# Gated mix of dilated attention and a gated MLP: another order of the first loads, ones for the early matmuls, and another split of the last tile

## The chip, the cores and the metric

The kernel runs on one core of one Trainium2 chip. The metric is the time of one execution on the device in microseconds (us). The time before is the median of three executions. Times inside an execution come from one profiled execution and are counted from the start of its span, that is from its first instruction.

## The reference

Everything is in bfloat16, for 2048 rows of 1024 columns (x). Two branches are computed from x and mixed by a gate.

```python
x = A_x
g = _sigmoid((x * gate_w).sum(-1, keepdims=True))
a = _A_ref(x, A_wqkv, A_wo)                  # 32 heads, 8 keys at a distance of 2, softmax, then wo
b = _B_ref(x, B_w_in, B_w_sp, B_b_sp, B_w_out)
return g * a + (1 - g) * b
...
z = _gelu(jnp.einsum('bsd,df->bsf', x, w_in))       # w_in: 1024 x 3584
z1 = z[..., :Fh].copy()
z2 = _layernorm(z[..., Fh:], axis=-1)
g = jnp.einsum('ts,bsf->btf', w_sp, z2) + b_sp[None, :, None]
return jnp.einsum('bsf,fd->bsd', z1 * g, w_out)
```

## The kernel before

The rows are 16 tiles of 128, the 1024 columns of x are 8 k tiles of 128. TensorE goes through these stages, one after the other: the second half of z (z2) for the first column blocks, q, k and v (L447), the rest of z2 (L232), the first half of z (L483), the spatial product g (L497) in four chunks, and after the chunks the two output products, attention (L510) and MLP (L520). The attention itself is done by VectorE beside the matmuls. PSUM has eight banks, taken in turn; ScalarE and VectorE copy results out of them.

The order of instructions on every engine is that of the program text: the scheduler is switched to manual, and each engine's queue executes in order. A small class, Beat, counts the columns that TensorE has multiplied and places VectorE's attention steps and some DMAs by that count. All DMAs before the change are issued from SP's queue; each issue takes the queue some tenths of a microsecond, and each DMA uses one of eight semaphores in turn, so that it also waits for the DMA that had the semaphore before.

The steps that the change touches are the first and the last.

At the start, matmuls on x need x transposed (columns on the partitions). For row tiles 2 to 15 the DMA transposes (L412). For row tiles 0 and 1 the plain tiles are loaded (L405, one DMA of 128 x 1024 each) and TensorE transposes them (L247): for each row tile two banks of four 128x128 transposes, each bank copied to xT in two parts, one by VectorE (L251) and one by ScalarE (L253). Behind the x tiles SP issues the eight k tiles of w_in for the first 1024 columns of z2 (L407, 256 KB each), then the transposing loads. At the very start VectorE clears a tile named warm (L87), and TensorE does six 128x512 matmuls on it whose result nobody reads (L92). Then comes the quad (z2_quad): both row tiles by both 512-column blocks in four PSUM banks, with the k tile as the outer loop, so that the work on a k tile starts when this tile has landed. ScalarE applies GELU to the four banks after the last k tile (L237). The row tiles 2 to 15 follow with the first column block, then v's weights are reordered (L218, L219), and the qkv stage starts with four weight blocks that SP loads at L205.

At the end, final_chunk(3) computes row tiles 12 to 15. For each column part of a row tile, attn_mm does 8 matmuls, mixer_mm 14, and combine does one operation on ScalarE (L527, attention times the gate, into one of two buffers asb) and one on VectorE (L528). The row tiles up to 14 have two parts of 512 columns and one store (L550); row tile 15 has parts of 512, 256 and 256 columns and a store after each (L548).

The constant that the change uses is one of four that the framework sets up in every program, with a one-column memset on GpSimd before the barrier at the start of the kernel (line L585 of the profile).

Of the kernel before, what the change touches and what calls it, by code (L numbers as in the profile page):

```python
# [11 lines left out]
BF = mybir.dt.bfloat16  # L12

P = 128
# [11 lines left out]
FH = 1792  # L26
NF = FH // P
ZC = 512
# [23 lines left out]
def kernel(  # L52
# [13 lines left out]
    nc = tc.nc  # L66
# [4 lines left out]
    sm = ctx.enter_context(tc.tile_pool(name="small", bufs=1))  # L71
    psum = ctx.enter_context(tc.tile_pool(name="psum", bufs=8, space=bass.MemoryType.PSUM))
# [4 lines left out]
    def reg(off, n):  # L77
        return arena[:, off:off + n]
# [4 lines left out]
    z1_d = dpool.tile([4, P, NF * 512], BF, name="z1_d")  # L83
    o_d = dpool.tile([S, D], BF, name="o_d")

    warm = sm.tile([P, 512], BF, name="warm")
    nc.vector.memset(warm[:], 0.0)  # L87

    def warm_up(n):
        pw = psum.tile([P, 512], F32, name="pw", tag="ps")  # L90
        for _ in range(n):
            nc.tensor.matmul(pw[:], warm[:, 0:P], warm[:], start=True, stop=True)  # L92

    ident = sm.tile([P, P], BF, name="ident")
    make_identity(nc, ident[:])
# [3 lines left out]
    for jh in range(2):  # L99
        for w in range(W):  # L100
            n = min(8, max(0, 14 - 2 * w - 8 * jh))
# [5 lines left out]
    gl_s = sm.tile([P, 16], F32, name="gl_s")  # L107
# [14 lines left out]
    xn = reg(A_OFF, 2 * D).rearrange("p (i d) -> p i d", i=2)  # L122
    z2 = reg(Z_OFF, 16 * FH).rearrange("p (i f) -> p i f", i=16)
    xT = reg(X_OFF, KT * S).rearrange("p (k s) -> p k s", k=KT)
# [10 lines left out]
    asb_slots = [reg(A_OFF + 14336 + r * 1024, 1024).bitcast(F32) for r in range(2)]  # L135
    w2 = reg(CD_OFF, KT * W2P).rearrange("p (k c) -> p k c", k=KT)
# [14 lines left out]
    x_v = x2.rearrange("(i q) d -> q i d", q=P)  # L151
# [3 lines left out]
    win_v = B_w_in.rearrange("(k p) c -> p k c", p=P)  # L155
    wsp_v = B_w_sp.rearrange("(a t) s -> a t s", t=P)
    wo_v = A_wo.rearrange("(g h d) n -> g h d n", g=NG, h=HG, d=DH)
    sync = nc.sync
# [72 lines left out]
    def z2_mm(ps, i, c, kt, N):  # L231
        nc.tensor.matmul(ps[:, 0:N], xT[:, kt, i * P:(i + 1) * P], w2[:, kt, ZC * c:ZC * c + N],  # L232
                         start=(kt == 0), stop=(kt == KT - 1))

    def z2_out(ps, i, c):
        n = ZW[c]
        nc.scalar.activation(z2[:, i, ZC * c:ZC * c + n], ps[:, 0:n], ACT.Gelu_apprx_tanh,  # L237
                             accum_out=s1[:, 4 * i + c:4 * i + c + 1])
        if c == 3:
            nc.scalar.copy(gl_s[:, i:i + 1], ps[:, n:n + 1])  # L240

    def z2_quad():
        for i in range(2):
            for h in range(2):
                pt = psum.tile([P, 4, P], BF, name="pt", tag="ps")
                for k in range(4):
                    nc.tensor.transpose(pt[:, k, :], xn[:, i, (4 * h + k) * P:(4 * h + k + 1) * P], ident[:])  # L247
                for k in (0, 2):
                    dst = xT[:, 4 * h + k:4 * h + k + 2, i * P:(i + 1) * P]
                    if k == 0:  # L250
                        nc.vector.tensor_copy(dst, pt[:, k:k + 2, :])  # L251
                    else:
                        nc.scalar.copy(dst, pt[:, k:k + 2, :])  # L253
        quad = [[psum.tile([P, 512], F32, name="ps", tag="ps") for c in range(2)] for i in range(2)]
        for kt in range(KT):
            for i in range(2):
                for c in range(2):
                    z2_mm(quad[i][c], i, c, kt, ZW[c])
        for i in range(2):
            for c in range(2):  # L260
                z2_out(quad[i][c], i, c)
        beat.run(2 * KT * (ZW[0] + ZW[1]))
# [105 lines left out]
    def load_oT(a):  # L368
        sync.dma_start_transpose(oT_slots[a % 3], o_d[a * P:(a + 1) * P, :])
# [31 lines left out]

    tc_order = ctx.enter_context(tc.manual_schedule())

    for i in range(2):
        sync.dma_start(xn[:, i, :], x_v[:, i, :])  # L405
    for kt in range(KT):
        sync.dma_start(w2[:, kt, 0:2 * ZC], win_v[:, kt, FH:FH + 2 * ZC])  # L407
    for i in range(2, 16):
        if i == 14:
            load_w(0, 2)  # L410
# [8 lines left out]
        sync.dma_start(w2[:, :, ZC * c:ZC * c + ZW[c]], win_v[:, :, FH + ZC * c:FH + ZC * c + ZW[c]])  # L419
    sync.dma_start(w2[:, :, FH:FH + 1], gw_v)  # L420

    warm_up(6)
    z2_quad()
    for i in range(2, 16):
        if i == 14:
# [13 lines left out]
    for ch in range(NCH):  # L439
# [3 lines left out]
        for j in range(NJ):  # L443
            ps = psum.tile([P, 512], F32, name="ps", tag="ps")
            for kt in range(KT):
                lhsT = _sub_ap(xT_flat, kt * S + j, [[NJ, P]])
                nc.tensor.matmul(ps[:].rearrange("p (t c) -> p t c", t=4), lhsT, wgt[:, :, kt, :],  # L447
                                 start=(kt == 0), stop=(kt == KT - 1))
# [25 lines left out]
    for f in range(NF):  # L474
# [5 lines left out]
        for c in range(4):  # L480
            ps = psum.tile([P, 512], F32, name="ps", tag="ps")
            for kt in range(KT):
                nc.tensor.matmul(ps[:], w1[:, kt, (f % 4) * P:(f % 4 + 1) * P], xT[:, kt, 512 * c:512 * (c + 1)],  # L483
                                 start=(kt == 0), stop=(kt == KT - 1))
# [22 lines left out]
    def attn_mm(a, n0, nw):  # L507
        psa = psum.tile([P, 512], F32, name="psa", tag="ps")
        for kt in range(KT):
            nc.tensor.matmul(psa[:, 0:nw], oT_slots[a % 3][:, kt, :], wo_sb[:, kt, n0:n0 + nw],  # L510
                             start=(kt == 0), stop=(kt == KT - 1))
        beat.run(KT * nw)
        return psa

    def mixer_mm(a, n0, nw):
        z1c = z1c_slots[a // 4 % 2]
        aa = a % 4
        psb = psum.tile([P, 512], F32, name="psb", tag="ps")
        for f in range(NF):
            nc.tensor.matmul(psb[:, 0:nw], z1c[:, f, aa * P:(aa + 1) * P], w_out_sb[:, f, n0:n0 + nw],  # L520
                             start=(f == 0), stop=(f == NF - 1))
        beat.run(NF * nw)
        return psb

    def combine(a, n0, nw, psa, psb):
        asb = asb_slots[n0 // nw % 2][:, 0:nw]
        nc.scalar.activation(asb, psa[:, 0:nw], ACT.Copy, scale=g_s[:, a:a + 1])  # L527
        nc.vector.scalar_tensor_tensor(ob_slots[a % 3][:, n0:n0 + nw], psb[:, 0:nw], omg[:, a:a + 1], asb,  # L528
                                       ALU.mult, ALU.add)

    def final_chunk(c):
        first = {}
        if c == 0:
            for a in range(2):
                for n0 in (0, 512):
                    first[a, n0] = mixer_mm(a, n0, 512)
            beat.flush(1e9)
        for a in range(4 * c, 4 * c + 4):
            ob = ob_slots[a % 3]
            if a > 0 and a + 2 < 16:  # L540
                load_oT(a + 2)
            last = a == 15
            for n0, nw in ((0, 512), (512, 256), (768, 256)) if last else ((0, 512), (512, 512)):
                psa = attn_mm(a, n0, nw)
                psb = first[a, n0] if (a, n0) in first else mixer_mm(a, n0, nw)
                combine(a, n0, nw, psa, psb)
                if last:
                    sync.dma_start(out2[a * P:(a + 1) * P, n0:n0 + nw], ob[:, n0:n0 + nw])  # L548
            if not last:
                sync.dma_start(out2[a * P:(a + 1) * P, :], ob)  # L550
# [10 lines left out]
    for aa in range(4):  # L561
        load_wsp(3, aa)
    final_chunk(0)
    load_z1c(2)
    g_chunk(2)
    final_chunk(1)
    load_z1c(3)
    g_chunk(3)
    final_chunk(2)
    final_chunk(3)  # L570

# [29 lines left out]
```

## Time and profile before

| what | us |
|---|---|
| median of 3 executions | 715.98 (715.62 to 716.28) |
| the profiled execution | 715.91 |
| its span, first to last instruction | 714.1 |
| TensorE matmul busy (PE) | 706.3 |
| VectorE (DVE) / ScalarE (ACT) busy | 413.9 / 246.1 |
| DMA: data moved, mean rate | 92.89 MB, 130 GB/s |
| granted TensorE clock, mean | 1.000 |

The page lists busy time per engine, the granted clock in 40 slices, the chain of work that ended last (followed back from the last instruction, with the share of each engine), and groups of instructions by program line. PE is TensorE's matmuls, PEld its weight loads, SPq the queue of the sync engine that issues DMAs. In a line of the timeline the columns are start, length, engine, line, operation, what it writes and reads, the count of merged instructions, and in brackets the idle time before it with what ended it. In a line of the chain they are start, length and what held the chain. A DMA's line gives its size and the time from the issue to the landing.

### The profile page before, as it was taken

Reading aid. Unit: us, or ns where it says so; the run is one execution under the profiler, and the core shown is the slowest. Engines: PE = TensorE matmul, PEld = TensorE weight load, DVE = VectorE, ACT = ScalarE, POOL = GpSimd, SP = SyncE. Lnnn points to the kernel's source line nnn. Section 1 sums busy time; section 2 is a strip of 40 time slices with the busy share of each in tenths; the row PEclk is TensorE's granted clock in tenths of the full one; section 3 lists DMA queues with packets and bytes.
Section 4 is the critical chain, followed back from the end, with each engine's and each line's share of the span. In section 5 each row is a group of like instructions: output and inputs, shape, how many; then the busy total and the mean of one; then the engine's idle time right before and its main releaser. Section 6 shows DMA issues by size and latency. Waiting matters only on the chain.

```text
span 714.1 us, 8323 instructions
## 1 busy us (share of the span) xinstructions
PE 706.3 (99%) x3321; PEld 365.5 (51%) x3372; DVE 413.9 (58%) x429; ACT 246.1 (34%) x451; POOL 14.0 (2%) x23
## 2 busy tenths in 40 slices
PE   8999999999999999999999999999999999999998
PEld 4466666666655554444444444444444444444444
DVE  0000589999999999999999999611222112221111
ACT  4434544435379886353331221111111111111111
POOL 1000000000000211000000000000000000000000
PEclk9999999999999999999999999999999999999999
DMA  9984974885673035974449880592400213002210
GB/s 234 187 182 105 255 197 102 205 200 161 172 200 131 0 115 108 223 252 144 173 150 255 298 167 8 179 183 66 132 1 0 57 49 116 1 1 59 60 45 30
DMA packets 176759, 92.89 MB, mean 130 GB/s; under 512 B 145104, under 2 KB 166992, under 8 KB 176208
## 3 DMA queue, kind: packets, MB, share of 16 engines
q1 hardware_dynamic: 176720, 92.36, 49.1%
q8 instruction: 26, 0.43, 0.3%
q14 instruction: 13, 0.11, 0.0%
HBM read 47.71 MB, written 28.38 MB: 107 GB/s over the span
## 4 chain that ended last, share of the span: by engine, by line
PE 98%; DMA 1%; issue 0%; SPq 0%; DVE 0%; DVEq 0%
PE ps L497 27%; PE ps L447 23%; PE ps L232 14%; PE ps L483 13%; PE psb L520 13%; PE psa L510 8%; DMA arena<-in_B_w_in_dram 1%; SPq L405 0%; DVE arena L528 0%; DVEq L528 0%
## 5 line engine op out<-in xcount | busy, mean ns | idle before, releaser
L497 PE MATMUL ps<-arena 128*128 128x512 bf16 x877 | 192.9, 379 | 1.0
L447 PE MATMUL ps<-arena 128*128 128x512 bf16 x768 | 165.9, 379 | 0.0
L497 PEld LDWEIGHTS <-arena 128*128 128x128 bf16 x896 | 87.7, 98 | 105.7
L447 PEld LDWEIGHTS <-arena 128*128 128x128 bf16 x768 | 110.7, 144 | 55.1
L520 PE MATMUL psb<-arena 128*128 128x512 bf16 (+1 forms) x455 | 100.9, 372 | 0.3
L275 DVE TENSOR_TENSOR arena<-arena 128x8192 bf16<-128x8192 bf16 x16 | 70.8, 4423 | 51.7 <-DMA arena<-k_d 51.4
L232 PE MATMUL ps<-arena 128*128 128x512 bf16 (+1 forms) x501 | 96.7, 352 | 1.4 <-DMA arena<-in_B_w_in_dram 0.9
L528 DVE SCALAR_TENSOR_TENSOR arena<-psb,omg,arena 128x512 bf16<-128x512 f32 (+1 forms) x33 | 24.3, 735 | 125.4 <-PE psb L520 101.5
L483 PE MATMUL ps<-arena 128*128 128x512 bf16 x439 | 96.4, 379 | 0.5
L501 ACT CAST arena<-ps 128x512 bf16<-128x512 f32 x56 | 32.8, 585 | 162.2 <-PE ps L497 136.6
L450 ACT CAST arena<-ps 128x512 bf16<-128x512 f32 x96 | 55.7, 586 | 93.0 <-PE ps L447 88.5
L278 DVE TENSOR_TENSOR arena<-arena 128x4096 bf16<-128x4096 bf16 (+1 forms) x64 | 77.5, 1210 | 1.9
L232 PEld LDWEIGHTS <-arena 128*128 128x128 bf16 x512 | 50.1, 98 | 47.8 <-issue 1.0
L520 PEld LDWEIGHTS <-arena 128*128 128x128 bf16 x462 | 45.2, 98 | 51.5
L308 DVE TENSOR_TENSOR arena<-arena,att_A 128x8192 bf16<-128x8192 bf16 x16 | 70.7, 4422 | 0.3
L483 PEld LDWEIGHTS <-arena 128*128 128x128 bf16 x448 | 43.8, 98 | 52.7
L502 DVE TENSOR_TENSOR arena<-arena 128x512 bf16<-128x512 bf16 x56 | 23.6, 422 | 71.7 <-ACT arena L501 71.7
L527 ACT ACTIVATE arena<-psa,g_s 128x512 f32<-128x512 f32 (+1 forms) x33 | 22.2, 674 | 122.3 <-PE psa L510 118.2
L510 PE MATMUL psa<-arena 128*128 128x512 bf16 (+1 forms) x259 | 59.6, 372 | 0.3
L485 ACT ACTIVATE arena<-ps 128x512 bf16<-128x512 f32 x56 | 32.2, 597 | 51.9 <-PE ps L483 41.1
L237 ACT ACTIVATE arena<-ps 128x512 bf16<-128x512 f32 (+1 forms) x64 | 34.3, 538 | 24.8 <-PE ps L232 23.6
L510 PEld LDWEIGHTS <-arena 128*128 128x128 bf16 x264 | 25.8, 98 | 29.7
(54 smaller groups left out, 257.4 us busy)
## 6 DMA issues: line engine op xcount, KB each, us to landing
arena<-k_d SPq DMA_DIRECT2D x8, 960.0 KB, 7.3
arena<-v_d SPq DMA_DIRECT2D x8, 960.0 KB, 5.1
z_d<-arena SPq DMA_DIRECT2D x14, 512.0 KB, 3.6
arena<-z_d SPq DMA_DIRECT2D x4, 1792.0 KB, 7.3
arena<-in_A_wqkv_dram SPq DMA_DIRECT2D x24, 256.0 KB, 4.6
arena<-in_B_w_in_dram SPq DMA_DIRECT2D x4, 1024.0 KB, 6.7
q_d<-arena SPq DMA_DIRECT2D x32, 128.0 KB, 2.3
k_d<-arena SPq DMA_DIRECT2D x32, 128.0 KB, 2.3
```

What stands on the lines that cost most here:

```text
L232: nc.tensor.matmul(ps[:, 0:N], xT[:, kt, i * P:(i + 1) * P], w2[:, kt, ZC * c:ZC * c + N], start=(kt == 0), stop=(kt == KT - 1))
L237: nc.scalar.activation(z2[:, i, ZC * c:ZC * c + n], ps[:, 0:n], ACT.Gelu_apprx_tanh, accum_out=s1[:, 4 * i + c:4 * i + c + 1])
L275: TT(prod.rearrange("p (w j c) -> p w j c", w=W, j=8, c=C), in0, in1, ALU.mult)
L278: return lambda: TT(pv[:, :, 0:half], pv[:, :, 0:half], pv[:, :, half:2 * half], ALU.add)
L308: TT(prod.rearrange("p (w j d h) -> p w j d h", w=W, j=8, d=DH, h=HG), in0, in1, ALU.mult)
L447: nc.tensor.matmul(ps[:].rearrange("p (t c) -> p t c", t=4), lhsT, wgt[:, :, kt, :], start=(kt == 0), stop=(kt == KT - 1))
L450: nc.scalar.copy(st[:, j % 4, :], ps[:])
L483: nc.tensor.matmul(ps[:], w1[:, kt, (f % 4) * P:(f % 4 + 1) * P], xT[:, kt, 512 * c:512 * (c + 1)], start=(kt == 0), stop=(kt == KT - 1))
L497: nc.tensor.matmul(ps[:], z2[:, i, f * P:(f + 1) * P], wsp[:, i, :, :].rearrange("p a t -> p (a t)"), start=(i == 0), stop=(i == 15))
L501: nc.scalar.copy(gsb, ps[:])
L510: nc.tensor.matmul(psa[:, 0:nw], oT_slots[a % 3][:, kt, :], wo_sb[:, kt, n0:n0 + nw], start=(kt == 0), stop=(kt == KT - 1))
L520: nc.tensor.matmul(psb[:, 0:nw], z1c[:, f, aa * P:(aa + 1) * P], w_out_sb[:, f, n0:n0 + nw], start=(f == 0), stop=(f == NF - 1))
```

## The change

Four edits, all at the two ends of the kernel:

- The first two row tiles of x are loaded as two column halves (128 x 2 x 512 each) instead of two row tiles; the second half is issued by SP after k tile 2 of w_in. Their transposes are split likewise: the four k tiles of the first half before the quad (two banks), those of the second half inside it, between the two row tiles of k tile 3.
- k tiles 1, 3, 5 and 7 of w_in are issued from ScalarE's queue. Ahead of them ScalarE copies 16 columns of ones into gl_s, which the gate overwrites later; ScalarE's first table load stands in front of this copy, as it stood in front of its first copy before.
- The early matmuls read the framework's constant of ones, repeated by its access pattern, instead of a cleared tile, and there is a seventh, of 128 columns. The memset on VectorE is gone.
- The last row tile has parts of 512, 384 and 128 columns; the buffer for ScalarE's result alternates with the part instead of going by its start column.

The order of all other instructions on the five engines is the same as before. In the built program SP issues the first half of x, k tiles 0 and 2, the second half, k tile 4 and k tile 6; k tile 6 waits for the landing of k tile 0 and the first transposing load for that of k tile 1, k tile 7 on ScalarE for that of the first half of x (they reuse those semaphores).

```diff
-    warm = sm.tile([P, 512], BF, name="warm")
-    nc.vector.memset(warm[:], 0.0)
-
-    def warm_up(n):
+    ones = nc.const_aps.tensor(1.0, [P, 512], BF)
+
+    def warm_up(widths):
         pw = psum.tile([P, 512], F32, name="pw", tag="ps")
-        for _ in range(n):
-            nc.tensor.matmul(pw[:], warm[:, 0:P], warm[:], start=True, stop=True)
+        for n in widths:
+            nc.tensor.matmul(pw[:, 0:n], ones[:, 0:P], ones[:, 0:n], start=True, stop=True)
...
+    def x_transposes(h):
+        for i in range(2):
+            pt = psum.tile([P, 4, P], BF, name="pt", tag="ps")
+            for k in range(4):
+                nc.tensor.transpose(pt[:, k, :], xn[:, i, (4 * h + k) * P:(4 * h + k + 1) * P], ident[:])
+            for k in (0, 2):
+                dst = xT[:, 4 * h + k:4 * h + k + 2, i * P:(i + 1) * P]
+                if k == 0:
+                    nc.vector.tensor_copy(dst, pt[:, k:k + 2, :])
+                else:
+                    nc.scalar.copy(dst, pt[:, k:k + 2, :])
...
     def z2_quad():
-        for i in range(2):
-            for h in range(2):
...
+        x_transposes(0)
         quad = [[psum.tile([P, 512], F32, name="ps", tag="ps") for c in range(2)] for i in range(2)]
         for kt in range(KT):
             for i in range(2):
+                if kt == 3 and i == 1:
+                    x_transposes(1)
                 for c in range(2):
                     z2_mm(quad[i][c], i, c, kt, ZW[c])
...
-    for i in range(2):
-        sync.dma_start(xn[:, i, :], x_v[:, i, :])
+    def load_x(h):
+        sync.dma_start(xn[:, :, 512 * h:512 * (h + 1)], x_v[:, 0:2, 512 * h:512 * (h + 1)])
+
+    load_x(0)
+    nc.scalar.copy(gl_s[:], ones[:, 0:16])
     for kt in range(KT):
-        sync.dma_start(w2[:, kt, 0:2 * ZC], win_v[:, kt, FH:FH + 2 * ZC])
+        if kt == 3:
+            load_x(1)
+        queue = nc.scalar if kt % 2 else sync
+        queue.dma_start(w2[:, kt, 0:2 * ZC], win_v[:, kt, FH:FH + 2 * ZC])
...
-    warm_up(6)
+    warm_up((512,) * 6 + (128,))
     z2_quad()
...
-    def combine(a, n0, nw, psa, psb):
-        asb = asb_slots[n0 // nw % 2][:, 0:nw]
+    def combine(a, n0, nw, slot, psa, psb):
+        asb = asb_slots[slot][:, 0:nw]
...
-            for n0, nw in ((0, 512), (512, 256), (768, 256)) if last else ((0, 512), (512, 512)):
+            for part, (n0, nw) in enumerate(((0, 512), (512, 384), (896, 128)) if last else ((0, 512), (512, 512))):
                 psa = attn_mm(a, n0, nw)
                 psb = first[a, n0] if (a, n0) in first else mixer_mm(a, n0, nw)
-                combine(a, n0, nw, psa, psb)
+                combine(a, n0, nw, part % 2, psa, psb)
```

## The prediction

> **What bounds the kernel now.** I read the page first, then the chain of work that ended last, then both ends of the span in the timeline. The page's busy rows, clock row and chain row:
>
> ```profile
> PE 706.3 (99%) x3321; PEld 365.5 (51%) x3372; DVE 413.9 (58%) x429; ACT 246.1 (34%) x451; POOL 14.0 (2%) x23
> ...
> PEclk9999999999999999999999999999999999999999
> ...
> PE 98%; DMA 1%; issue 0%; SPq 0%; DVE 0%; DVEq 0%
> ```
>
> TensorE is the bound, at full granted clock, with no hole between its first real matmul and its last. So only three things can move the time: when the first real matmul starts, what is put into TensorE's stream, and what follows its last matmul. The chain over the first 40 us shows the first of these:
>
> ```profile
> 0.74 0.39 SPq L405
> ...
> 1.19 0.42 SPq L405
> ...
> 1.64 4.40 DMA arena<-in_B_w_in_dram
> ...
> 6.09 5.99 PE ps L232 x27
> ```
>
> The first k tile of w_in (w0 below) is issued at 1.64 and lands at 6.05; the quad's first matmul starts at 6.09. From there the end is 705 us away, whatever happens off TensorE. What stands before it, in the timeline of the first 20 us:
>
> ```profile
> 0.86 0.27 DVE L87 MEMSET warm<- 128x256 uint32 x1 [0.86 <-PEq L585]
> ...
> 1.19 2.74 PE L92 MATMUL pw<-warm 128*128 128x512 bf16 x6 [1.19 <-DVE warm L87]
> ...
> 3.72 1.51 PE L247 MATMUL pt<-ident,arena 128*128 128x128 bf16 x16
> ...
> 4.39 1.17 DVE L251 COPY arena<-pt 128x256 bf16<-128x256 bf16 x4 [3.26 <-PE pt L247]
> ```
>
> All 16 transposes are done by 5.23, in the shade of w0: they cost nothing today. The issues asked for one at a time (KB each, us to landing) are row tile 0, row tile 1, w0, w1, and the last wqkv block of the first group:
>
> ```profile
> arena<-in_A_x_dram SPq DMA_DIRECT2D x1, 256.0 KB, 2.7
> ...
> arena<-in_A_x_dram SPq DMA_DIRECT2D x1, 256.0 KB, 3.0
> ...
> arena<-in_B_w_in_dram SPq DMA_DIRECT2D x1, 256.0 KB, 4.4
> ...
> arena<-in_B_w_in_dram SPq DMA_DIRECT2D x1, 256.0 KB, 4.6
> ...
> arena<-in_A_wqkv_dram SPq DMA_DIRECT2D x1, 256.0 KB, 4.9
> ```
>
> With their issue times (0.74, 1.19, 1.64, 2.12, 31.43) they land at 3.4, 4.2, 6.05, 6.7 and 36.3. The later w tiles follow to w7 at 10.8 (issued 5.12, 5.7 us): 4.8 us for seven, 0.68 each, while TensorE uses one in four matmuls of 0.216 us, 0.86. So after w0 TensorE never waits. The end of the chain:
>
> ```profile
> 709.52 1.54 PE psb L520 x14
> ...
> 711.16 0.48 DVE arena L528
> ```
>
> then a 64 KB store (issued at 711.67, 1.6 us to landing) and the closing semaphores, to 714.1.
>
> **The change, part by part.** All sums are against the profiled execution: 715.91 us, 1.8 more than its span of 714.1. The median shown (715.98) is 0.07 above it; I add that at the end.
>
> *Ones for the early matmuls.* The memset of 0.27 us on VectorE goes, and its wait. ScalarE's first instruction starts at 0.73; the first early matmul can start about there instead of 1.19. Six at 0.427 (weight loads at 1.59, 2.02, 2.44) and one of a quarter of that are 2.67 us: they end at 3.41, where x lands. Worth nothing by itself; the transposes wait for x. It does matter for speed: in the transposes of today eight start in the 0.85 us from 3.70 (107 ns each), and from 4.65 on they stand 56 ns apart. Full speed came 3.46 us after the first early matmul. By the same interval it comes at 4.2.
>
> *Halves of x.* The first 256 KB now hold half of both row tiles, so w0 needs 256 KB ahead of it in SP's queue, not 512. It takes row tile 1's place: issue at 1.19 (the x issue of 1 KB rows at 0.39, as today's 2 KB rows, or up to 0.58 as a wqkv issue of 256 B rows). **Earliest landing:** that of row tile 1 today, 4.23. Then the transposes decide: eight from 3.72 at 0.107 end at 4.57, the first copy out of PSUM runs 4.39 to 4.68 as now, and the quad can start at 4.75.
>
> *Odd k tiles from ScalarE's queue.* SP issues one every 0.47 us and they land every 0.68, so the issue isn't what limits them: no gain in rate. The order of arrival changes, though. If ScalarE's first issue runs while its table load (1.28 us from 0.73) is under way, w1 and w3 start beside x and w0, and w0 is third or fourth in line. **Latest landing:** where the third or fourth transfer lands today, 6.05 (w0) to 6.72 (w1). If ScalarE issues only after the table load and the small copy, from about 2.1, w0 is in front. The trace of before has no DMA on ScalarE, so it doesn't tell. I take 5.15, the middle of 4.23 and 6.05, and a quad start of 5.2: a gain of **0.9**, between 1.34 and a loss of 0.67.
>
> The Trainium skill speaks against this part: "DMA: Bandwidth & Descriptors", section "Issuing engines are not separate DMA queues", says that DMAs issued from different engines run on the same 16 DMA engines and interleave, and that only issue time is saved. By it alone w0 would be at the late end of the bounds.
>
> ScalarE's four issues are about 1.9 us; behind them stand the PSUM copies of L253, now first at 4.72. The fourth issue reuses the semaphore of x's first half (3.4) and would end near 3.9: covered by 0.8 us. Without that cover, k tiles 2 and 3 come late, and TensorE with them by the same amount. SP's next w tile waits for w0, the first transposed row tile for w1. Row tile 2 lands at 12.0 now (6.06 + 5.9) and is needed at 13.0; the eight w tiles ahead of it are unchanged in bytes. An hour-glass further on: TensorE reaches the first wqkv matmul at 37.17, the last block lands at 36.3. Whatever the start gains beyond 0.88 is lost there, unless those loads come forward.
>
> *Second half of the transposes.* Eight now stand inside the quad, after k tile 3's first row tile: 8 x 0.056 = **0.45** on the path, no longer in w0's shade. Their copies (0.29 on VectorE) lie beside two matmuls (0.43) of k tile 3; nothing waits for them longer. x's second half must be there 14 matmuls in, at 8.2. As the fifth transfer it lands like w2 now (7.6), as the seventh like w4 (8.9); but it is seventh only if ScalarE issues early, and then the quad starts later too (9.1). I take no wait; at worst 0.7.
>
> *Tail.* 44 matmuls of 256 columns at 0.109 become 22 of 384 (0.162, between 0.109 and 0.216) and 22 of 128 (0.056, the late transposes): 4.80 and 4.81. VectorE's last operation shrinks from 0.48 at 256 columns; with 0.75 at 512 that is 0.35 at 128: **-0.13**. The ScalarE half is finished before. The last store is 32 KB in 256 B rows; the q_d stores, also in 256 B rows, take 2.3, the last one 1.6: 0 to 0.7, I take 0. Tail -0.12, between -0.25 and +0.5. The buffer index of the ScalarE result alternates now; both orders write a buffer that VectorE has left.
>
> **Sum:** -0.9 + 0.45 - 0.12 = -0.57: 715.34 for the profiled execution, 715.4 as a median. With the ends of w0 alone: 4.75 gives -1.01 (715.0), 6.76 gives +1.0 (717.0).
>
> **Rivals.**
> - *The queues share.* ScalarE's issues run at once, w0 lands at 6.05 to 6.72 and the transposes are a bare cost: +0.3 to +1.0, 716.3 to 717.0. For it: semaphore waits of ScalarE's queue are executed while a table load runs (the last at 358.9, within the load of 357.87 to 359.15), so the queue runs ahead of the engine. Against it: the early transfers could use a first stretch (1.6 to 2.6) that moves only 170 GB/s, against 359 in the next us.
> - *Slower, by the clock.* Early matmuls and transposes fill TensorE from 0.74 to 4.57 only if x comes on time. If full speed isn't there when the quad starts, each matmul costs 0.427 instead of 0.216. From 10 of them the sum of -0.57 turns into +1.5; 16 give +2.8: 717.5 to 718.8. Against it: 2.74 us of early matmuls and eight transposes were enough today.
> - *Faster than the sum.* Full speed at 4.2 brings the first eight transposes nearer to 56 ns: the quad starts at 4.35 with w0 at 4.23, and the wqkv loads come forward, since SP has four fewer issues: -1.74 + 0.45 - 0.12 = -1.41, 714.4 to 714.6.
>
> On the clock the skill has a harder rule: "TensorE: Matmul & The Clock Gate", "Part 4: PE-mode transpose", says that transposes don't count as busy, and Part 1 asks for some 3.4 us of sustained work. By it 2.67 us are too little, and the clock rival would be the forecast; today's 2.74 us, with full speed at 4.65, speak against that.
>
> **How the numbers follow.** A measurement of this kernel can tell about 0.2% (1.4 us) from no change: 714.55 and 717.4 are the bounds. Forecast (715.0 to 716.0): 0.50. Queues share (716.0 to 717.0): 0.32. Clock: 0.08. Faster than the sum: 0.10. The first two are both within 0.2%, so same 0.82, faster 0.10, slower 0.08. The range holds the first two and the edge of the last: 714.6 to 717.0.
>
> **What would show it.** The quad's first matmul at 5.2 (4.75 to 5.6 for the forecast, 6.1 and later for sharing); ScalarE's first DMA issue near 2.1 (forecast) or before 1.3 (sharing); 56 ns between the transposes inside the quad, 0.216 between all its matmuls; no idle of TensorE before the first L447 matmul; 0.35 for the last VectorE operation. A w tile that TensorE waits for after the first would make the sum wrong.

## The result and the profile after

| | us |
|---|---|
| median after, 11 executions | 717.79 (716.37 to 718.86) |
| median before, 11 executions beside them | 716.10 (715.39 to 716.79) |
| ratio | 1.0027, 95% interval 1.0019 to 1.0036 |
| profiled execution after (its span) | 718.86 (717.1) |

The change made the kernel slower by 0.27%, more than the 0.2% that a measurement can tell; the forecast was 715.4 within 714.6 to 717.0. The profiled execution is the slowest of its eleven, so its 2.95 us over the profiled execution before show more of the mechanism than the median's 1.69 do.

The page's busy rows (share of the span, instructions) and clock row of the kernel after:

```profile
PE 711.7 (99%) x3373; PEld 365.2 (51%) x3373; DVE 413.7 (58%) x428; ACT 246.7 (34%) x452; POOL 14.0 (2%) x23
...
PEclk9999999999999999999999999999999999999999
```

TensorE's busy time is 5.4 us up, but that is not the loss: the row of before lacks some fifty matmul records (3321 against 3372 weight loads). The clock row shows nothing: a slice is 18 us long, and the trace's own record of the clock begins with its first change (the opening, at 11.27 in this trace), so every view reads 1.00 ahead of it, in the kernel before too. The speed of a first stretch is read from the distances of the matmuls. The chain of the first 45 us (start, length, what held it):

```profile
1.25 5.07 DMA arena<-in_B_w_in_dram
...
6.37 5.59 PE ps L231 x14
11.96 0.45 PE pt L245 x8
12.40 28.06 PE ps L231 x130
```

w0 is the second issue in SP's queue now, at 1.25 instead of 1.64, and takes 5.07 instead of 4.40. The quad starts at 6.37 (6.09 before). Then fourteen matmuls take 5.59 us: 0.40 each, where full speed gives 0.216 (a 128x512 matmul, start to start). The timeline of the first 20 us shows why (idle time before and its end in brackets):

```profile
0.73 1.28 ACT L411 ACT_TABLE_LOAD   x1 [0.73 <-PEq L594]
0.74 0.46 SPq L408 DMA_DIRECT2D arena<-in_A_x_dram  x1
...
0.77 2.83 PE L91 MATMUL pw<-const-bfloat16-1.0 128*128 128x512 bf16 x7 [0.77 <-PEq L594]
0.79 1.42 ACTq L416 DMA_DIRECT2D arena<-in_B_w_in_dram  x3
...
5.22 1.03 PE L245 MATMUL pt<-ident,arena 128*128 128x128 bf16 x8 [1.62 <-DMA arena<-in_A_x_dram]
...
8.03 0.15 PEld L231 LDWEIGHTS <-arena 128*128 128x128 bf16 x1 [0.28 <-issue]
8.45 0.15 PEld L231 LDWEIGHTS <-arena 128*128 128x128 bf16 x1 [0.28 <-issue]
```

ScalarE issues its three loads from 0.79 on, while its table load runs. x lands late, and TensorE sits idle for 1.62 us between the early matmuls and the first transpose. The weight loads of the quad then stand 0.42 apart (8.03, 8.45): each matmul runs at half speed. They come closer after 11.01 (the next at 11.36), where the clock opened; 12 matmuls were slow. Three of the DMAs (KB each, us from issue to landing):

```profile
arena<-in_A_x_dram SPq DMA_DIRECT2D x1, 256.0 KB, 4.4
...
arena<-in_B_w_in_dram ACTq DMA_DIRECT2D x1, 256.0 KB, 4.2
...
arena<-in_B_w_in_dram SPq DMA_DIRECT2D x1, 256.0 KB, 5.1
```

These are x's first half (issued 0.74, landed 5.18), w1 (0.79, 4.98) and w0 (1.25, 6.33). Before, row tile 0, as many bytes issued at the same time, landed at 3.42. The end of the chain after, with the last VectorE operation at 0.35 instead of 0.48:

```profile
713.40 0.80 PE psb L529 x14
...
714.29 0.35 DVE arena L537
```

The sum for the two profiled executions: quad's start +0.28; 12 slow matmuls, 2.40 in excess; eight transposes inside the quad, +0.447; from the last matmul's start to the end 3.11 instead of 3.35, -0.24. Together 2.89 of the 2.95 measured. For the median, +0.28 + 0.45 - 0.24 = 0.49 leaves 1.2 of the 1.69 for the slow matmuls, an estimate: some six of them in place of twelve.

### The profile page after: what moved, and what is told of

It is laid out like the page before. It is cut to its first block, busy times and chain, and to the rows that moved or that the text cites. A ratio compares the mean times of both kernels' runs of the same rounds, so it can differ in the third digit from the quotient of the medians.

```text
span 717.1 us, 8378 instructions
## 1 busy us (share of the span) xinstructions
PE 711.7 (99%) x3373; PEld 365.2 (51%) x3373; DVE 413.7 (58%) x428; ACT 246.7 (34%) x452; POOL 14.0 (2%) x23
## 4 chain that ended last, share of the span: by engine, by line
PE 99%; DMA 1%; SPq 0%; DVE 0%; issue 0%; DVEq 0%
PE ps L506 27%; PE ps L456 23%; PE ps L231 14%; PE psb L529 13%; PE ps L492 13%; PE psa L519 8%; DMA arena<-in_B_w_in_dram 1%; SPq L408 0%; PE pt L245 0%; DVE arena L537 0%; DVEq L537 0%
## 5 line engine op out<-in xcount | busy, mean ns | idle before, releaser
L529 PE MATMUL psb<-arena 128*128 128x512 bf16 (+2 forms) x462 | 101.6, 373 | 0.0
L231 PE MATMUL ps<-arena 128*128 128x512 bf16 (+1 forms) x512 | 99.9, 358 | 0.1
L537 DVE SCALAR_TENSOR_TENSOR arena<-psb,omg,arena 128x512 bf16<-128x512 f32 (+2 forms) x33 | 24.2, 735 | 125.3 <-PE psb L529 109.4
L536 ACT ACTIVATE arena<-psa,g_s 128x512 f32<-128x512 f32 (+2 forms) x33 | 22.3, 675 | 122.9 <-PE psa L519 122.9
L519 PE MATMUL psa<-arena 128*128 128x512 bf16 (+2 forms) x264 | 60.0, 373 | 0.0
```

## The experiments

One theory and its rivals. *Sharing closes the clock*: ScalarE's early loads delay x, the hole that this leaves in TensorE's work keeps the clock closed, and slow matmuls are the loss. The rivals: the constant (other data or another start for the early matmuls), the 1 KB rows of the halves by themselves, or the new tail. Below, "before" is the median of the kernel before, run on the same chip beside the kernel in question; it lies between 715.63 and 716.01, so a time is best compared with its own "before".

### One part at a time

**All issues from SP** (e1_all_sp):

```diff
-        queue = nc.scalar if kt % 2 else sync
-        queue.dma_start(...)
+        sync.dma_start(...)
```

> The changed kernel with all eight w_in tiles issued by SP again (order: first half of x, w0, w1, w2, second half of x, w3 to w7); everything else as changed. Theory 'shared DMA engines': ScalarE's loads w1, w3 and w5 are what delayed the first half of x from 3.4 to 5.2, TensorE stood idle for 1.6 us and so began the quad at half clock. Then x lands at 3.4 to 3.7 here, the quad starts at 4.75 to 5.3, at most 4 quad matmuls stand 427 ns apart, and the time is 0.3 to 1.0 us below the kernel before. Rival 'constant': matmuls on a constant do not open the clock; then 10 or more quad matmuls are still at 427 ns and the time is 1 us or more above before. Rival 'halves': the 1 KB rows themselves land late; then x lands at 4.5 or later.

715.77 (715.10 to 716.34), before 715.84, ratio 0.9998 (0.9989 to 1.0008). The slow matmuls are gone, and so is the loss; the gain of 0.3 to 1.0 that was expected did not appear. PE's timeline of this kernel:

```profile
3.63 0.76 PE L245 MATMUL pt<-ident,arena 128*128 128x128 bf16 x8
4.55 2.82 PE L231 MATMUL ps<-arena 128*128 128x512 bf16 x12 [0.16 <-DVE arena L249]
8.55 0.59 PE L231 MATMUL ps<-arena 128*128 128x512 bf16 x2 [1.18 <-DMA arena<-in_B_w_in_dram]
```

x lands at 3.59 and the quad starts at 4.55, 1.54 earlier than before, at full speed. Twelve matmuls later TensorE waits for k tile 3 (8.51): x's second half, which stands ahead of it in the queue, landed 1.71 after w2. The early start of 1.54 pays for a wait of 1.40 and 0.45 of transposes. The halves of x by themselves cost x little: 3.59 against 3.42.

**The kernel before with the odd k tiles on ScalarE** (e2_queue_only):

```diff
+    nc.scalar.copy(gl_s[:], ones[:, 0:16])
...
-        sync.dma_start(...)
+        queue = nc.scalar if kt % 2 else sync
+        queue.dma_start(...)
```

> The kernel before with one part of the change alone: w1, w3, w5, w7 from ScalarE's queue behind a table load and a 16-column copy of ones. Shared DMA engines: row tile 0 lands near 5.0 instead of 3.4, the quad starts at 6.5 to 7.3 and 8 to 16 of its matmuls are at 427 ns: 1 to 3 us above before. Rivals 'constant' and 'halves' (neither part is in it): within 0.3 us of before.

718.76 (718.54 to 720.02, 5 executions), before 715.84, ratio 1.0046 (1.0034 to 1.0059): by this edit alone the loss of the whole change, and more. PE's timeline:

```profile
4.16 1.04 PE L249 MATMUL pt<-ident,arena 128*128 128x128 bf16 x8 [0.23 <-DMA arena<-in_A_x_dram]
5.50 1.03 PE L249 MATMUL pt<-ident,arena 128*128 128x128 bf16 x8 [0.30 <-DMA arena<-in_A_x_dram]
7.16 13.16 PE L234 MATMUL ps<-arena 128*128 128x512 bf16 x53 [0.62 <-DMA arena<-in_B_w_in_dram]
```

x's first row tile lands at 4.12 (3.42 before) and w0 at 7.12, 1.07 later than before. TensorE has holes of 0.23, 0.30 and 0.62 us on the way there, and eight slow matmuls after them (1.55 in excess).

**A cleared tile instead of the constant** (e3_cleared_tile):

```diff
-    ones = nc.const_aps.tensor(1.0, [P, 512], BF)
+    warm = sm.tile([P, 512], BF, name="warm")
+    nc.vector.memset(warm[:], 0.0)
```

> The changed kernel with the early matmuls on a tile cleared by VectorE instead of the constant of ones (same seven matmuls, about 0.4 us later). Shared DMA engines: x still lands near 5.2 and the quad begins at half clock: within 0.6 us of the changed kernel, 1.2 to 2.5 us above before. Rival 'constant': the clock is open when the quad starts, and the time falls to that of before plus 0.6 at most.

717.58 (716.07 to 718.25), ratio 1.0018 (1.0008 to 1.0027): the loss stays, so the constant is not its cause. The eleven times fall into two groups, 716.07 to 716.31 (three) and 717.28 to 718.25 (eight). The profiled execution is of the lower group (716.21); its PE timeline:

```profile
4.98 0.62 PE L248 MATMUL pt<-ident,arena 128*128 128x128 bf16 x8 [0.95 <-DMA arena<-in_A_x_dram]
6.13 3.18 PE L234 MATMUL ps<-arena 128*128 128x512 bf16 x14 [0.53 <-DMA arena<-in_B_w_in_dram]
```

x is late here too (4.94), and fourteen matmuls take 3.18, not 5.59. So with such holes the clock opens in time in some executions. That it separates the two groups is likely, not shown: the upper one has no profile.

**The hole filled** (e4_long_early), four more early matmuls:

```diff
-    warm_up((512,) * 6 + (128,))
+    warm_up((512,) * 10 + (128,))
```

> The changed kernel with ten early matmuls of 512 columns and one of 128 instead of six and one, so that TensorE is busy from 0.77 until x lands near 5.2. Shared DMA engines with the clock: no hole before the transposes, full speed is there when the quad starts at 6.3 or within 5 of its matmuls, so 1.2 to 2.2 us below the changed kernel, and 0 to 0.7 above before (the bare cost of the late w0 and the transposes in the quad). Rival 'constant': the clock opens no earlier than 11 us and the time is that of the changed kernel.

716.40 (716.16 to 716.63), ratio 1.0008 (1.0000 to 1.0017). PE's timeline:

```profile
0.77 4.53 PE L91 MATMUL pw<-const-bfloat16-1.0 128*128 128x512 bf16 x11 [0.77 <-PEq L594]
...
6.16 3.28 PE L231 MATMUL ps<-arena 128*128 128x512 bf16 x14
```

The loads are those of the kernel after and nearly as late (x at 4.95, w0 at 6.11); with no hole every matmul of the quad but the first has full speed. The time is 0.56 above its own "before", where the kernel after is 1.69 above, so filling the hole is worth 1.1 (1.39 if the medians 717.79 and 716.40 are set against each other). The spread of eleven executions falls from 2.5 to 0.47. In the profile there stay the quad's start (+0.07), the transposes (+0.45), the first matmul, ahead of the clock's opening at 6.39 (+0.10), and the tail (-0.24): 0.38.

**The tail alone** (e5_tail_only), the kernel before with 512, 384, 128:

```diff
-            for n0, nw in ((0, 512), (512, 256), (768, 256)) if last else ((0, 512), (512, 512)):
+            for part, (n0, nw) in enumerate(((0, 512), (512, 384), (896, 128)) if last else ((0, 512), (512, 512))):
```

> The kernel before with the last part of the change alone: the last row tile in parts of 512, 384 and 128 columns. The changed kernel's profile has 0.35 us for the last VectorE operation instead of 0.48 and 0.22 us longer from the last store's issue to the end: the price by the prediction is -0.12, by that profile 0.0 to 0.1. A rival that looks for the loss at the end needs +1 us or more here. Theory 'shared DMA engines and clock': within 0.2 us of before.

715.77 (715.32 to 716.31), before 715.98, ratio 0.9994 (0.9986 to 1.0003). The medians differ by 0.21, the tail in the profile by 0.31 (3.35 to 3.04); the interval holds no change as well.

**The constant alone** (e6_ones_only):

```diff
-    warm = sm.tile([P, 512], BF, name="warm")
-    nc.vector.memset(warm[:], 0.0)
+    warm = nc.const_aps.tensor(1.0, [P, 512], BF)
```

> The kernel before with the early matmuls on the constant of ones alone (six of 512 columns, from about 0.77 instead of 1.19). Shared DMA engines and clock: the data arrive as before, the first row tile near 3.4, and the hole between the early matmuls (end 3.4) and the transposes (3.7) stays small: w0 decides the quad's start at 5.2 to 6.1, at most 5 quad matmuls at 427 ns, time within 0.5 us of before. Rival 'constant': 10 or more quad matmuls at 427 ns, 2 us above before.

715.74 (715.29 to 717.55), ratio 0.9998 (0.9989 to 1.0006). The early matmuls start at 0.77, the clock opens at 3.82. In the profiled execution, the shortest of the twelve, the quad starts at 5.47, so the span was 0.62 shorter, but the median isn't.

**No early matmuls** (e10_no_early), the kernel before without its line `warm_up(6)`, to price the clock:

> The kernel before without its six early matmuls (their result is read by nobody). It prices the clock alone: data arrive as before, the quad starts at 5.3 to 6.5, TensorE was busy only with the 16 transposes from 3.5 on, so 8 to 24 quad matmuls stand at 427 ns: 1.7 to 5.1 us above before. If the clock were not what early matmuls are about, the time would be that of before within 0.3 us.

716.95 (715.86 to 719.24), ratio 1.0020 (1.0009 to 1.0031). The profiled execution (718.80) has 12 slow matmuls, 2.48 us in excess, as the kernel after has. The median lost 1.15 against 715.80, less than the 1.7 to 5.1 expected, and the times spread over 3.4 us: the lowest (715.86) is as fast as the median with early matmuls. Without them an early opening of the clock is left to chance, and the early matmuls make it likely.

The Trainium skill, "TensorE: Matmul & The Clock Gate", "Part 1: The HAM clock gate", says the same: the clock follows a window of some 3.4 us that runs free, so that one kernel sees another number of slow matmuls in each execution.

The traces agree, and say more. Where TensorE had no hole of over 0.4 us by then, full speed came 2.8 to 5.9 us after the first early matmul (2.79 in e16_all_sp_again, 3.48 before, 5.62 with the hole filled, 5.87 in e7_held below). With the hole of 1.62 it came at 11.27, in e2_queue_only at 10.35. Every stretch of the clock's record between two changes is a whole number of windows of 3.413 us (6.83 open and 3.41 closed in e9_late_half below, 709.97 open before). Such windows, laid back from the first opening, had TensorE at work (each matmul and transpose taken up to the start of the next one) for 73% (e13_equal_rows below) to 100% where they ended with the clock open, and for 72% (e7_held) or less where they left it closed: in the kernel after 1.03 to 4.45 with 69% and 4.45 to 7.86 with 68%. Transposes count in this: in e11_ones_tail and e5_tail_only the opening windows had matmuls of 512 columns for 40% and 41% of them, with the transposes 88% and 91%.

From this follows an estimate for the kernel after, made with the results known. If a window ends between 3.2 and 4.35, the early matmuls (0.77 to 3.40) open the clock before the quad: a third of all phases. In six of ten it opens between 8.0 and 10.1, for 0.8 to 1.8 us in slow matmuls, and in the rest at 11.2 to 11.4, for 2.4. From 716.46 (718.86 less 2.40) that gives 716.5, 717.3 to 718.3 and 718.8 to 718.9. Of the eleven times one is 716.37, eight lie from 717.37 to 718.23, two are 718.82 and 718.86. By this estimate it is the phase of the windows that decides what an execution loses, and the median is one of the middle group; no run sets the phase, so it isn't tested by itself.

### Can the early start be kept?

**ScalarE held until x is there** (e7_held). A small store of x's first row, which has to wait for x, stands ahead of ScalarE's loads:

```diff
+    nc.scalar.dma_start(hold_d[:, :], xn[0:1, 0, 0:64])
...
-        queue = nc.scalar if kt % 2 else sync
+        queue = nc.scalar if kt in (1, 3, 5) else sync
```

> The changed kernel with w1, w3 and w5 still issued by ScalarE, but held back until the first half of x has landed: a store of 64 elements of it to a scratch row, which nothing reads, goes ahead of them on ScalarE's queue and waits for x. w7 goes to SP. If it is the loads beside x that made x late, the first half of x lands at 3.4 to 3.7 and w0 near 4.4, the quad starts at 4.5 to 4.9, and w1 (issued near 4.1) lands at 5.8 to 7.0, so TensorE waits for it once by 0.5 to 1.5 us: 0.5 below to 0.8 above before. If the use of ScalarE's queue is slow by itself, x still lands at 4.5 or later and the time is that of the changed kernel.

719.51 (717.60 to 721.24, 6 executions), ratio 1.0055 (1.0041 to 1.0068), 3.5 above before, where 0.8 was the most expected. x lands at 3.59 and the quad starts at 4.63, so the delay of x does come from the loads beside it. But w1, issued at 4.14, lands at 8.38, after all that SP issued up to 3.61; TensorE waits for it after four matmuls:

```profile
4.63 1.89 PE L231 MATMUL ps<-arena 128*128 128x512 bf16 x4
8.42 2.32 PE L231 MATMUL ps<-arena 128*128 128x512 bf16 x10 [1.90 <-DMA arena<-in_B_w_in_dram]
```

This is the fastest of the six executions; the other five, 719.38 and more, have no profile, so what they lost beyond this wait is not shown.

**x's second half from ScalarE, late** (e9_late_half); SP issues w0 to w4, w6 and w7, and ScalarE, held in the same way, x's second half and w5:

```diff
+    for kt in (0, 1, 2, 3):
+        load_w2(kt, sync)
+    load_x(1, nc.scalar)
+    load_w2(4, sync)
...
```

> A version meant to beat both: ones and new last row tile; SP issues the first half of x, w0 to w4, w6 and w7; ScalarE, held by a store of 64 elements until the first half of x has landed, issues only what is needed late: the second half of x and w5. Theory: nothing lies beside x and w0, so x lands near 3.6, w0 near 4.4 and the quad starts at 4.5 to 4.8 at full speed or within 5 matmuls of it; w1 to w3 land in order, 0.7 apart, and the second half of x at 6.5 to 8.0. Without a stall TensorE reaches the qkv stage at 36.0 to 36.4 (before 37.2): 0.5 to 1.3 us below before. If one transfer is late by 1.2 us wherever it is placed, as in all runs with loads from SP alone, TensorE waits for it and the gain is 0 to 0.4.

716.83 (716.45 to 719.27), ratio 1.0016 (1.0007 to 1.0026). In the profiled execution (718.75, the second slowest) the transfer issued at 4.06 took 5.9 us to land, TensorE waited for it 14 matmuls in, and eight slow matmuls followed the wait. PE's timeline, and the row of the window from 11 to 14 us (length, busy time of each engine, granted clock, DMA share, GB/s):

```profile
4.41 3.29 PE L231 MATMUL ps<-arena 128*128 128x512 bf16 x14 [0.16 <-DVE arena L249]
10.05 0.62 PE L245 MATMUL pt<-ident,arena 128*128 128x128 bf16 x8 [2.35 <-DMA arena<-in_A_x_dram]
```

```profile
11.00:14.00 3.00, 3.00 (x9) 1.07 (x8) 0.00 (x1) 1.74 (x3) 0.00 (x0) 0.50 1.10 212
```

The clock had been open from 3.73 and closed at 10.56, at the end of the window with the hole, for 3.41 us. TensorE was at work for 26% of that window; in e7_held, a window with 48% left the clock open.

**Constant and tail, without the loads** (e11_ones_tail), the two edits of e5_tail_only and e6_ones_only together, and the same with two more early matmuls between the transposes and the quad (e8_filled):

```diff
         for i in range(2):
...
+        warm_up(2)
```

> The kernel before with the two parts of the change that cost nothing: the ones (six early matmuls from 0.77) and the last row tile in 512, 384, 128; loads and transposes as before. Theory: start as before, tail 0.24 us shorter as in the profiles of the kernels that have it (3.11 from the last matmul's start to the end of the span against 3.35), full speed 0.4 us earlier: 0.1 to 0.6 us below before. Rival: the constant or the tail costs something: at or above before.

> The kernel before with the ones, the new last row tile, and two more early matmuls of 512 columns between the transposes and the quad, where TensorE waits for w0; loads as before. By the theory of the clock TensorE is busy without a hole of more than 0.4 us from 0.77 until the quad: all runs have full speed at the quad's start, the spread of the runs falls under 0.8 us (before: 1.4 us over eleven runs), and the median is 0.1 to 0.6 us below before. If the clock plays no part in the spread of before, the median stays within 0.15 us and the spread as it was.

715.67 (715.09 to 718.26), ratio 1.0007 (0.9997 to 1.0016), and 715.87 (715.62 to 716.42), ratio 0.9999 (0.9991 to 1.0008). Neither is a gain that can be told. Three of eleven executions are above 717 without the two matmuls, none above 716.42 with them: what a filled hole should do, but three of eleven are too few to show it. In both profiles the earlier quad (5.78, 5.44) ran into a wait for a later w tile (0.68, 0.86).

### What makes x late

**One load on ScalarE** (e12_one_load):

```diff
-        queue = nc.scalar if kt % 2 else sync
+        queue = nc.scalar if kt == 5 else sync
```

> The changed kernel with one load on ScalarE's queue (w5, issued near 0.8) instead of four; w1, w3 and w7 from SP. If each load that lies beside x takes its share of the DMA engines, the first half of x lands between e1's 3.6 (none) and the changed kernel's 5.2 (three): 4.0 to 4.5, the hole of TensorE is 0.5 to 1.0 us, and the time lies between those two kernels, 0 to 1.2 us above before. If only the number of transfers ahead in SP's own queue counts, x lands at 3.6.

717.90 (716.27 to 718.08, 6 executions), ratio 1.0031 (1.0019 to 1.0043). x lands at 5.10, not at the 4.0 to 4.5 expected: one neighbour of 256 KB costs x as much as three. In the profiled execution (716.27, the lowest of six) the clock was open all the same, though TensorE had idled 1.55 us:

```profile
5.15 0.62 PE L245 MATMUL pt<-ident,arena 128*128 128x128 bf16 x8 [1.55 <-DMA arena<-in_A_x_dram]
```

**That load in rows of 1 KB** (e13_equal_rows):

```diff
+            for c in range(2):
+                nc.scalar.dma_start(w2[:, kt, ZC * c:ZC * (c + 1)], win_v[:, kt, FH + ZC * c:FH + ZC * (c + 1)])
```

> The kernel with one load on ScalarE's queue, and that load (k tile 5 of w_in) cut into two of 128x512, whose rows are 1 KB like those of x's column half. If the two queues are served row by row, so that rows of 2 KB beside rows of 1 KB take two thirds of the rate, equal rows leave x half of it: x's first half lands at 4.1 to 4.5 us (2 KB beside 2 KB landed at 4.12), and TensorE's idle time before the first transpose is 0.6 to 0.9. If any neighbour on a second queue at the start costs about the same, x lands at 4.9 to 5.2 as with the uncut load (5.10).

One execution, 716.09. x lands at 4.57, just above the 4.1 to 4.5 of row by row and well below the 4.9 to 5.2 of any neighbour. (The first of the two loads beside x also has half the bytes of the uncut one; the run doesn't separate that from the rows.) PE's timeline:

```profile
4.61 0.62 PE L245 MATMUL pt<-ident,arena 128*128 128x128 bf16 x8 [1.01 <-DMA arena<-in_A_x_dram]
```

The first 256 KB of x landed so: rows of 2 KB alone 3.2 to 3.4, beside 2 KB rows 4.12; rows of 1 KB alone 3.5 to 3.6, beside 1 KB rows 4.57, beside 2 KB rows 4.94 to 5.18. The packets agree: between 3.0 and 4.0 us the kernel after moved 99 packets of 1 KB for x and 74 of 2 KB for ScalarE, the kernel e2_queue_only 89 and 98 of 2 KB each. In these runs the queues are served roughly packet by packet, and who has the shorter rows gets the smaller share. That isn't all of it: the first two microseconds of data are slower with two queues. Of the kernel after and of e1_all_sp, busy time and the data moved (GB/s, last column) in the window 1.6 to 2.6:

```profile
1.60:2.60 1.00, 1.00 (x4) 0.42 (x3) 0.00 (x0) 0.62 (x2) 0.84 (x13) 1.00 0.29 83
```

```profile
1.60:2.60 1.00, 1.00 (x4) 0.42 (x3) 0.00 (x0) 0.62 (x2) 0.83 (x13) 1.00 0.51 165
```

From 2.6 to 3.6 it is 221 and 327. Rows of unequal length are not the reason: e13_equal_rows moved 116 and 185. With x in rows of 2 KB the loss is absent (156 and 332 in e2_queue_only). Why the second queue slows the first microseconds of the short rows stays open.

### The place of x's second half

**All from SP, the second half after k tile 3** (e14_sp_later_half):

```diff
-        if kt == 3:
+        if kt == 4:
             load_x(1)
-        queue = nc.scalar if kt % 2 else sync
-        queue.dma_start(...)
+        sync.dma_start(...)
```

> All loads from SP, and the second column half of x after k tile 3 of w_in instead of before it; constant, transposes in two parts and last tile as in the kernel after. If the wait that ate the early start (1.40 us, for k tile 3, behind x's second half) belongs to that place in the order, the quad starts at 4.4 to 4.7, waits 0.1 to 0.9 in all, and the time is 0.4 to 1.2 below the kernel before. If one transfer in the first ten us is late by about 1.2 us whichever it is, it falls on another tile and the time is that of the kernel with all loads from SP: within 0.3 of the kernel before.

715.36 (714.69 to 715.93), before 716.01, ratio 0.9987 (0.9978 to 0.9996). The same kernel again, beside the kernel of e1_all_sp, both on one chip:

> The same kernel as the one with x's second half after k tile 3 (all loads from SP), beside the kernel with that half after k tile 2. If the place of the half decides, it is again 0.3 to 1.0 below the kernel before and 0.2 to 1.0 below its neighbour, with the quad's waits below 0.5 us. If the first result was the chance of its session, both are within 0.3 of the kernel before and of each other.

> All loads from SP with x's second half after k tile 2, as measured before (within 0.3 of the kernel before, TensorE waiting 1.4 us for k tile 3). If the place of the half decides, that wait is seen again (0.8 to 1.6 us). If one transfer in the first ten us is late by chance, whichever it is, the wait can be missing or stand at another k tile.

With the half after k tile 3: 715.38 (715.09 to 716.14), ratio 0.9995 (0.9986 to 1.0003). After k tile 2: 716.04 (715.82 to 716.33), ratio 1.0005 (0.9996 to 1.0013). Before: 715.63. PE's timeline of the one and then of the other:

```profile
4.57 3.19 PE L231 MATMUL ps<-arena 128*128 128x512 bf16 x14
8.03 0.62 PE L245 MATMUL pt<-ident,arena 128*128 128x128 bf16 x8 [0.26 <-DMA arena<-in_A_x_dram]
```

```profile
4.43 3.02 PE L231 MATMUL ps<-arena 128*128 128x512 bf16 x12 [0.21 <-DMA arena<-in_B_w_in_dram]
8.31 0.59 PE L231 MATMUL ps<-arena 128*128 128x512 bf16 x2 [0.86 <-DMA arena<-in_B_w_in_dram]
```

x's second half is late in both, by 1.4 us after the transfer ahead of it; behind it k tile 3 waits, and in front of it k tile 3 is there. The waits are 0.43 and 1.30 in all, the medians 0.66 apart: the place decides between these two. Against the kernel before, the later place is 0.65 below the first time, an interval just off 1, and 0.25 the second time, with an interval that holds 1: it is the fastest version here, by less than 0.2%, and a gain over the kernel before isn't settled.

## Why the prediction was wrong

| term | forecast | measured (profiled execution) |
|---|---|---|
| x's first half lands | 3.4 | 5.18 |
| w0 lands | 5.15 (4.23 to 6.05) | 6.33 |
| quad's start | 5.2, -0.9 | 6.37, +0.28 |
| slow matmuls in the quad | none | 12, +2.40 |
| transposes in the quad | +0.45 | +0.447 |
| tail | -0.12 | -0.24 |

- **The step that failed** is in "Ones for the early matmuls": "they end at 3.41, where x lands". The text then bounded the landing of w0 by sharing, 4.23 to 6.72, and left x where row tile 0 had landed, in every case. x is issued 0.05 us before ScalarE's first load and shares with it almost from its first packets (at 2.15 and 2.52). With x at 5.18 the early matmuls end 1.62 too soon.
- **The rivals were priced as strangers.** "The queues share" had +0.3 to +1.0 and 0.32; "Slower, by the clock" had 0.08: the text says that it needs x late, and no part of the sum made x late. The first brings about the second: e2_queue_only shows late loads and slow matmuls from the queue edit alone, e4_long_early that filling the hole takes 1.1 to 1.4 of the 1.69 back. Sharing by itself came out as priced: quad at 6.37 within 6.1 and later, 0.49 for the three terms without the clock, and a time of 716.4 in e4_long_early, within "716.3 to 717.0". The price of the clock was right as well: 0.211 for a slow matmul in the text, 2.40 for 12 in the profile, 0.20 each.
- **The clock itself.** The argument against slow matmuls, that 2.74 us of early matmuls and eight transposes "were enough today", left out that today they stand without a hole. The harder rule put beside it, that transposes don't count as busy, does not fit this case's traces (e11_ones_tail, e5_tail_only above); and 2.67 us of early matmuls are not always too little, but enough in about a third of the phases by the estimate above.
- **ScalarE's issue** was left open, "near 2.1 (forecast) or before 1.3 (sharing)". It came at 0.79, inside the table load of 0.73 to 2.01. The argument for it, that the queue runs ahead of the engine, was in the text and got the smaller chance. The argument against, that two queues might fill the slow first stretch, did not hold: that stretch fell from 170 to 83 GB/s (165 in e1_all_sp).
- **The rule that speaks against the change**, from the Trainium skill, "DMA: Bandwidth & Descriptors", "Issuing engines are not separate DMA queues", was weighed for w0 and not for x. That the transfers interleave is what the trace shows; that only issue time is saved leaves out that the first transfer pays for it, 3.6 to 5.18.
- **No wait behind w0** held with the late quad, in the kernel after and, at full speed, in e4_long_early. Where the quad did start early the step would have failed too: e1_all_sp started at 4.55, earlier than the forecast, and waited 1.40 for k tile 3. So an earlier quad would not have given the forecast's gain with the second half where the change has it.
- **Transposes and last operation** were right: 0.447 against 0.45, and 0.35 as forecast. The tail came out at -0.24 instead of -0.12: counted from the last matmul's start it also holds that matmul, which has 128 columns instead of 256.

## What to carry to other kernels

A DMA from a second queue at the very start was paid for here by the transfer that the start waits for, the more so with that transfer in shorter rows; keep the first load alone, and give each later one the place in which it is needed. Price rivals together when one can set off another: the late loads cost 0.3 by themselves and, through the hole of 1.6 us and the clock, up to 2.4 more. Where the first transfer can be late, let the early matmuls reach past it; four more cost nothing that could be told here and made executions alike (a spread of 2.5 us became 0.47).

## What was not expected of the hardware

- ScalarE's queue issues DMAs (0.79) while the engine's table load (0.73 to 2.01) runs, and its issue overlaps SP's: 0.74 to 1.20 on SP, 0.79 to 1.20 on ScalarE; SP's is as long as alone (0.46 in e1_all_sp).
- In every run with all loads on SP, at least one transfer among the first ten landed 1.07 to 2.35 us after the one before it, where most others follow at 0.6 to 0.9: w0 before (15 of its 16 parts had landed at 5.57, the last at 6.05), x's second half in three runs, other w tiles elsewhere. In e1_all_sp it took back most of what the earlier start gained. What it is stays open.
- One profile was a poor witness for a median: that of the kernel after is the slowest of its eleven executions, those of e3_cleared_tile and e12_one_load are among the fastest of theirs. The list of times told which.
